# Attention matmuls in 64-row halves of the TensorE array, with ScalarE and VectorE in program order

## The chip, the cores and the metric

One core of one Trainium2 chip runs the whole program. The metric is device time in microseconds (us), lower is better: the median of three runs of the kernel before is 1672.16 us (1672.11 to 1676.5).

## The reference

Eight sequences of 2496 tokens go through an attention without softmax, then all 19968 tokens through a soft mixture of experts. Everything is float32.

```python
scores = (1.0 / S) * np.matmul(z, z.transpose(0, 2, 1))   # z: 8 x 2496 x 64
attn = np.maximum(scores, 0.0) ** 2
x = u * np.matmul(attn, v)                                # u, v: 8 x 2496 x 256
...
logits = x.reshape(N, D) @ phi                            # phi: 256 x 32 (8 experts, 4 slots each)
d = exp(logits - logits.max(0)); d /= d.sum(0) + 1e-9     # over the tokens
slot_out[e] = np.maximum((d.T @ x)[e] @ w1[e], 0) @ w2[e]
c = exp(logits - logits.max(1)); c /= c.sum(1) + 1e-9     # over the slots
out = c @ slot_out
```

## The kernel before, in words

**Split numbers.** Float32 products are made from the fast type fp32r: a value is split in a high part (a copy cast to fp32r) and a low part (the value less the high one), and a product is the sum of high x high, high x low and low x high. A tile of z holds both parts in both halves of its 128 rows: slot 0 has the high part in rows 0 to 63 and the low part in rows 64 to 127, slot 1 the other way round (`load_z`, L55 to L63). A tile of v holds high and low side by side (`load_v`, L65 to L71; its low part is made on GpSimd for 35 of the 80 tiles, L70).

**Attention.** A step is one tile of 128 keys (`kt`, 20 of them) for one chunk of up to 512 queries (`ch`; five per sequence, four of 512 and one of 448 columns, and in the last sequence six, the last two of 256). `scores` (L134) makes a 128 x 512 tile of scores with two matmuls over all 128 rows (L141, L142: they give all four products, low x low too), ScalarE takes relu (L144) and square (L145), VectorE casts the high part `ph` (L147) and subtracts the low part `pl` (L150). `attend` (L156) then adds six matmuls over all 128 rows (keys) to the accumulator `acc`, two column halves c of v by three products (L163 four, L169 two). `scores` runs three steps ahead of `attend` (LOOKAHEAD). The last key tile has 64 real keys; its high and low parts share one tile, so it needs four matmuls in `attend`.

**Small steps.** A finished chunk is multiplied by u, split in `xh` and `xl` (`finish_chunk`, L178), and for each group of 512 tokens g a list `work` gets four `group_tile` calls (L201: transposition of 128 tokens and their logits in one matmul by `rmat`, `tr`, L209, then copies) and four stages of `group_soft` (L224: the running maximum over tokens by two transpositions, `cmT` L238 and `mbT` L250, exponentials L254, L271, L281, and the sums over the slots `sl`, eight matmuls L263 and L264). One entry of `work` is taken at each of eight places of a chunk (POPS).

**Order.** The Tile scheduler sets the order on each engine by priority; nothing is pinned but one pair (`issue_after`). PSUM: `acc` has two buffers of two banks, `sc` two of one bank, `ms` (the small steps) two of one bank.

**End.** The turning of the weights c (`turn`, L287), the expert layers (L405, L427) and the output (`tokens`, L473). The last are matmuls over 32 rows each, four of them in four different row strips of the array (L481), with their own weights, 512 columns wide, type fp32r.

Of the kernel before, what the change touches and what calls it, by code (L numbers as in the profile page):

```python
# [15 lines left out]
P = 128  # L16
# [11 lines left out]
LOOKAHEAD = 3  # L28
# [3 lines left out]
STAGES = 4  # L32
POPS = (3, 5, 7, 9, 11, 13, 16, 18)
# [5 lines left out]

@with_exitstack  # L40
def attn_soft_moe_kernel(ctx, tc, uT, v, zz, phi, ww, outT):
    nc = tc.nc

# [4 lines left out]
    ms_ps = mid_ps.enter_context(tc.tile_pool(name="ms_ps", bufs=2, space=PSUM))  # L48
# [3 lines left out]
    xpool = moe.enter_context(tc.tile_pool(name="xpool", bufs=1))  # L52


    def load_z(b, j):  # L55
        raw = raws.tile([P, 512], F32, tag="raw", name=f"zr_{b}_{j}")
        nc.sync.dma_start(raw, zz[b, :, j * 512 : (j + 1) * 512])
        t = blk.tile([P, 2, 512], F32R, tag="blk", name=f"z_{b}_{j}")
        for h in (1, 0):
            rows = slice(h * 64, (h + 1) * 64)  # L60
            (nc.vector.tensor_copy if h and b + j == 0 else nc.scalar.copy)(t[rows, h], raw[rows])
            nc.vector.tensor_sub(t[rows, 1 - h], raw[rows], f32(t[rows, h]))  # L62
        return t  # L63

    def load_v(b, i):  # L65
        raw = raws.tile([P, 2, D], F32, tag="raw", name=f"vr_{b}_{i}")
        nc.sync.dma_start(raw, v[b, :, 2 * i : 2 * i + 2, :])
        t = blk.tile([P, 2, 2, D], F32R, tag="blk", name=f"v_{b}_{i}")
        nc.scalar.copy(t[:, :, 0], raw)  # L69
        (nc.gpsimd if b and i > 4 else nc.vector).tensor_sub(t[:, :, 1], raw, f32(t[:, :, 0]))  # L70
        return t  # L71

    zt, vt_ = {(0, 0): load_z(0, 0)}, {}


    ident = cpool.tile([P, P], F32, name="ident")
    make_identity(nc, ident)


    esel = cpool.tile([2 * NS, E_, NS], F32, name="esel")  # L80
    rsel = cpool.tile([P, 2, 4, NS], F32, name="rsel")
    nc.gpsimd.memset(esel, 0.0)
    nc.gpsimd.memset(rsel, 0.0)
    for h in range(2):
        rows = slice(h * NS, (h + 1) * NS)
        nc.gpsimd.tensor_copy(
            esel[rows, :, 0:SE], ident[rows, rows].rearrange("k (e s) -> k e s", s=SE)
        )
        for r in range(4):
            nc.gpsimd.tensor_copy(  # L90
                rsel[:, h, r, 16 * h : 16 * h + 16].rearrange("k (j s) -> k j s", s=SE),
                ident.rearrange("k (j q) -> k j q", q=NS)[:, :, 0:SE],
            )
    phi_sb = xpool.tile([P, 2, NS], F32, name="phi_sb")
    nc.sync.dma_start(phi_sb, phi.rearrange("(c p) s -> p c s", p=P))
    rmat = xpool.tile([P, 2, 256], F32R, name="rmat")
    nc.vector.memset(f32(rmat), 0.0)
    for c in range(2):
        nc.vector.tensor_copy(rmat[:, c, 0:P], ident)
        nc.vector.tensor_copy(rmat[:, c, P : P + NS], phi_sb[:, c])  # L100
        nc.vector.tensor_sub(
            rmat[:, c, P + NS : P + 2 * NS], phi_sb[:, c], f32(rmat[:, c, P : P + NS])
        )


    NXT = 6
    xth = [xpool.tile([P, 258], F32R, name=f"xth{i}") for i in range(NXT)]
    xtl = [xpool.tile([P, 256], F32R, name=f"xtl{i}") for i in range(NXT)]
    for t in xth:
        nc.vector.memset(f32(t[:, 256:258]), 1.0)  # L110
    slot_acc = [cpool.tile([2 * NS, 258], F32, name=f"slot_acc{i}") for i in range(2)]
    runmax = [cpool.tile([2 * NS, 1], F32, name=f"runmax{i}") for i in range(2)]
    cw = cpool.tile([P, NG, P], F32, name="cw")
# [19 lines left out]

    pend = {}  # L134

    def scores(b, ch, kt):
        j, o, n, t0 = ch
        zk, zq = zt[b, kt // 4], zt[b, j]
        ps = sc_ps.tile([P, QC], F32, tag="sc", name=f"sc_{t0}_{kt}")
        lhs = zk[:, 0, (kt % 4) * P : (kt % 4 + 1) * P]  # L140
        nc.tensor.matmul(ps[:, :n], lhs, zq[:, 0, o : o + n], start=True, stop=False)  # L141
        nc.tensor.matmul(ps[:, :n], lhs, zq[:, 1, o : o + n], start=False, stop=True)  # L142
        r = wa.tile([P, QC], F32, tag="r", name=f"r_{t0}_{kt}", bufs=4)
        nc.scalar.activation(r[:, :n], ps[:, :n], AF.Relu, scale=1.0 / S)  # L144
        nc.scalar.activation(r[:, :n], r[:, :n], AF.Square)  # L145
        hi = wa.tile([P, QC], F32R, tag="ph", name=f"ph_{t0}_{kt}", bufs=5)
        nc.vector.tensor_copy(hi[:, :n], r[:, :n])  # L147
        if kt < KT - 1:
            lo = wa.tile([P, QC], F32R, tag="pl", name=f"pl_{t0}_{kt}", bufs=5)
            nc.vector.tensor_sub(lo[:, :n], r[:, :n], f32(hi[:, :n]))  # L150
        else:
            lo = None
            nc.vector.tensor_sub(hi[64:128, :n], r[64:128, :n], f32(hi[64:128, :n]))  # L153
        pend[t0, kt] = hi, lo

    def attend(b, ch, kt, acc):  # L156
        j, o, n, t0 = ch
        hi, lo = pend.pop((t0, kt))
        vt = vt_[b, kt // 2][:, kt % 2]
        last = kt == KT - 1  # L160
        for c in range(2):
            for h in range(2):
# [392 lines left out]
```

## Time and profile before

| what | value |
|---|---|
| profiled execution, its own time | 1676.33 us |
| its span, first to last instruction | 1674.6 us |
| runs | 1676.5, 1672.11, 1672.16 us |
| granted TensorE clock, mean | 0.986 |
| busy: PE, VectorE (DVE), ScalarE (ACT), GpSimd (POOL) | 1632.9, 1296.0, 1154.1, 58.4 us |
| matmuls, other instructions of note | 8155 matmuls, each with a weight load (PEld); 216 DMAs |
| HBM | 53 GB/s over the span |

How to read the profile's rows. A group row names line, engine, operation, output<-inputs, shape, xcount, then busy us, mean ns of one, and the idle time ahead of it with what ended it. A timeline row has the start in us from the span's start, the length, and xcount instructions merged. Matmuls are pipelined: a 512-column matmul is shown with about 390 ns, but the next one starts some 230 ns after it, so distances between starts are what counts. A row of windows has the length of a stretch and the busy time (and count) of each engine in it.

### The profile page before, as it was taken

What the parts mean: (1) busy time and instruction counts of PE and PEld (TensorE: products, weight loads), DVE (VectorE), ACT (ScalarE), POOL (GpSimd) and SP (SyncE); (2) the same over time, 40 slices, a digit from 0 to 9 for tenths busy, and PEclk for the clock granted to TensorE, in tenths of its full rate; (3) what the DMA queues carried; (4) which work ended last, traced back from release to release, by engine and by line L of the source; (5) the groups of instructions that cost most, each with busy time, mean ns of one, the idle gap of its engine ahead of it and who ended that gap; (6) DMA issues with size and microseconds to landing.
All of it is one profiled execution on the core that took longest, in us unless ns stands there. A gap on an engine that the chain in (4) does not pass through costs nothing.

```text
span 1674.6 us, 22717 instructions
## 1 busy us (share of the span) xinstructions
PE 1632.9 (98%) x8155; PEld 1347.3 (80%) x8155; DVE 1296.0 (77%) x2904; ACT 1154.1 (69%) x2191; POOL 58.4 (3%) x53
## 2 busy tenths in 40 slices
PE   8999999999999999999999999999999999999985
PEld 6788888888888888888888888888888889888953
DVE  8877977779777887779877797778977787777853
ACT  8766866678666776668666686667866676666743
POOL 0000100000000100001000010001000020000000
PEclk9999999999999999999999999999999999999985
DMA  5100310013000120002100030001200021000559
GB/s 158 51 14 12 89 44 14 11 32 89 13 14 12 57 63 14 13 12 77 44 13 14 18 100 27 14 12 45 76 13 14 12 81 63 13 15 12 182 222 389
DMA packets 36594, 90.63 MB, mean 54 GB/s; under 512 B 3713, under 2 KB 6273, under 8 KB 34433
## 3 DMA queue, kind: packets, MB, share of 16 engines
q1 hardware_dynamic: 36480, 89.18, 16.4%
q8 instruction: 64, 1.05, 0.3%
q14 instruction: 50, 0.40, 0.1%
HBM read 68.71 MB, written 20.45 MB: 53 GB/s over the span
## 4 chain that ended last, share of the span: by engine, by line
PE 88%; DVE 6%; ACT 2%; DMA 2%; issue 1%; SPq 0%; DVEq 0%; ACTq 0%
PE acc L163 40%; PE acc L169 19%; PE sc L141 10%; PE sc L142 10%; PE tr L209 4%; DVE pl L150 2%; DMA outT<-ot 2%; DVE ph L147 2%; PE sl L263 1%; PE sl L264 1%; DVE z L62 1%; ACT r L145 1%; ACT r L144 1%; PE h L405 1%; DVE ot L487 1%
## 5 line engine op out<-in xcount | busy, mean ns | idle before, releaser
L163 PE MATMUL acc<-ph,v 128*128 128x512 f32 (+2 forms) x3280 | 862.5, 385 | 0.3 <-DVE ph L153 0.3
L144 ACT ACTIVATE r<-sc 128x512 f32<-128x512 f32 (+2 forms) x820 | 471.5, 575 | 407.5 <-PE sc L142 402.9
L163 PEld LDWEIGHTS acc<-ph,v 128*128 128x128 f32 x3280 | 608.7, 188 | 123.3 <-DVE ph L153 0.7
L150 DVE TENSOR_TENSOR pl<-r,ph 128x512 fp32r<-128x512 f32 (+2 forms) x779 | 528.3, 679 | 23.8
L147 DVE CAST ph<-r 128x512 fp32r<-128x512 f32 (+2 forms) x820 | 345.8, 423 | 221.0 <-ACT r L145 210.4
L145 ACT ACTIVATE r<-r 128x512 f32<-128x512 f32 (+2 forms) x820 | 502.1, 612 | 16.8
L169 PE MATMUL acc<-pl,v 128*128 128x512 f32 (+2 forms) x1558 | 472.0, 384 | 0.0
L169 PEld LDWEIGHTS acc<-pl,v 128*128 128x128 f32 x1558 | 290.3, 188 | 57.8
L141 PE MATMUL sc<-z,z 128*128 128x512 f32 (+2 forms) x656 | 258.2, 394 | 0.0
L142 PE MATMUL sc<-z,z 128*128 128x512 f32 (+2 forms) x656 | 251.4, 383 | 0.0
L141 PEld LDWEIGHTS sc<-z,z 128*128 128x128 f32 x656 | 123.5, 188 | 21.8
L142 PEld LDWEIGHTS sc<-z,z 128*128 128x128 f32 x656 | 123.7, 189 | 17.2
L221 DVE TENSOR_TENSOR xtl<-tr,xth 128x256 fp32r<-128x256 f32 x156 | 65.5, 420 | 51.4 <-ACT xth L220 51.3
L70 POOL TENSOR_TENSOR v<-vr,v 128x512 fp32r<-128x512 f32 x35 | 55.7, 1605 | 1314.4 <-ACT v L69 942.3
L209 PE MATMUL tr<-rmat,xl 128*128 128x256 f32 x312 | 80.5, 281 | 0.0
L209 PE MATMUL tr<-rmat,xh 128*128 128x256 f32 x312 | 80.3, 280 | 0.0
L220 ACT CAST xth<-tr 128x256 fp32r<-128x256 f32 x156 | 57.4, 369 | 20.9 <-DVE lt L215 20.6
L141 PE MATMUL sc<-z 128*128 128x512 f32 (+2 forms) x164 | 65.9, 402 | 5.9 <-DVE z L62 4.7
L142 PE MATMUL sc<-z 128*128 128x512 f32 (+2 forms) x164 | 63.9, 390 | 0.3 <-DVE z L62 0.3
L209 PEld LDWEIGHTS tr<-rmat,xh 128*128 128x128 f32 x312 | 58.6, 188 | 5.8
L209 PEld LDWEIGHTS tr<-rmat,xl 128*128 128x128 f32 x312 | 58.5, 188 | 5.6 <-DVE xl L193 0.2
L191 DVE TENSOR_TENSOR x<-acc,ut 128x256 f32<-128x256 f32 (+7 forms) x72 | 52.3, 727 | 5.7 <-PE acc L163 5.7
(88 smaller groups left out, 954.3 us busy)
## 6 DMA issues: line engine op xcount, KB each, us to landing
vr<-in_v SPq DMA_DIRECT2D x80, 256.0 KB, 2.7
w<-in_w SPq DMA_DIRECT2D x32, 512.0 KB, 6.0
outT<-ot SPq DMA_DIRECT2D x16, 1024.0 KB, 8.4
ut<-in_uT SPq DMA_DIRECT2D x31, 512.0 KB, 3.7
zr<-in_zz SPq DMA_DIRECT2D x40, 256.0 KB, 2.6
ut<-in_uT SPq DMA_DIRECT2D x8, 448.0 KB, 3.4
outT<-ot SPq DMA_DIRECT2D x4, 512.0 KB, 5.1
outT<-ot SPq DMA_DIRECT2D x2, 768.0 KB, 6.0
```

What stands on the lines that cost most here:

```text
L70: (nc.gpsimd if b and i > 4 else nc.vector).tensor_sub(t[:, :, 1], raw, f32(t[:, :, 0]))
L141: nc.tensor.matmul(ps[:, :n], lhs, zq[:, 0, o : o + n], start=True, stop=False)
L142: nc.tensor.matmul(ps[:, :n], lhs, zq[:, 1, o : o + n], start=False, stop=True)
L144: nc.scalar.activation(r[:, :n], ps[:, :n], AF.Relu, scale=1.0 / S)
L145: nc.scalar.activation(r[:, :n], r[:, :n], AF.Square)
L147: nc.vector.tensor_copy(hi[:, :n], r[:, :n])
L150: nc.vector.tensor_sub(lo[:, :n], r[:, :n], f32(hi[:, :n]))
L163: nc.tensor.matmul(acc[:, c, :n], vt[:, h, c * P : (c + 1) * P], hi[:, :n], start=(kt == 0 and h == 0), stop=(last and h == 1),)
L169: nc.tensor.matmul(acc[:, c, :n], vt[:, 0, c * P : (c + 1) * P], lo[:, :n], start=False, stop=False,)
L209: nc.tensor.matmul(ps[:, c], xp[:, c, t * P : (t + 1) * P], rmat[:, c], start=(k == 0), stop=(k == 1))
L220: nc.scalar.copy(xth[i][:, 0:D].rearrange("p (c q) -> p c q", c=2), ps[:, :, 0:P])
L221: nc.vector.tensor_sub(xtl[i].rearrange("p (c q) -> p c q", c=2), ps[:, :, 0:P], f32(xth[i][:, 0:D]).rearrange("p (c q) -> p c q", c=2),)
```

## The change

Line numbers of the changed kernel are of no use below, since all its operations are recorded through one helper (L46), so tile names are used: `sc` scores, `ph`/`pl` high and low part of the squared scores, `acc` the accumulator, `tr`, `cmT`, `mbT`, `sl` the small steps.

1. **Scores.** Two key tiles at a time: tile h (0 or 1) uses rows 64h to 64h+63 of z only, with three matmuls over 64 rows (high x high, high x low, low x high; low x low is dropped). The two halves alternate, each into its own bank.
2. **Attend.** Four key tiles (p) at a time, in two passes s. Each matmul over 128 keys becomes two over 64 keys. In pass s the half h writes column half c = h XOR s, so that the two halves are always in different banks. Between the passes a GpSimd no-op waits for the last matmul of a pass, and the first matmul of the next pass waits for that no-op (`turns`, `await_`).
3. **Order.** Everything recorded through `pe`, `act`, `dve` keeps the order of the code. Ahead of each pass s stand one entry of `work` and the scores of the pair after (`pair(i + 1, s)`); three lists (`begin`, `middle`, `behind`) put each small ScalarE or VectorE step half a step after its input.
4. **Small steps.** `tr`, `cmT`, `mbT` in 64-row halves; `sl` in plain float32 as eight matmuls of 64 rows by 32 columns (four token tiles by two halves) instead of eight fp32r matmuls over 128 rows; `ms` has one buffer of two banks; logits and `xt` are copied by ScalarE; the low part of x for `sl` and its copies go away; the low part of v is made on VectorE always.
5. **Loads.** The DMAs stay on SP's queue in much the same places; the split of a loaded tile is put one load later (`landing`); at the start the constants come after the first scores.
6. The very last block of attention is done over 128 rows (`attend_whole`). The expert layers and the output are unchanged.

```diff
-    def scores(b, ch, kt):
+    def scores(b, ch, p, w):
...
-        nc.tensor.matmul(ps[:, :n], lhs, zq[:, 0, o : o + n], start=True, stop=False)
-        nc.tensor.matmul(ps[:, :n], lhs, zq[:, 1, o : o + n], start=False, stop=True)
+        for m, (kl, ql) in enumerate(((0, 0), (0, 1), (1, 0))):
+            for h, rows in enumerate(HALF):
+                c = 2 * w + h
+                pe.matmul(
+                    ps[h][:, :n], zk[rows, h ^ kl, c * P : (c + 1) * P],
+                    zq[rows, h ^ ql, o : o + n], start=(m == 0), stop=(m == 2),
+                )
+        rs = []
+        for h in range(2):
+            r = wa.tile([P, QC], F32, tag="r", name=f"r_{t0}_{k0 + h}", bufs=5)
+            act.activation(r[:, :n], ps[h][:, :n], AF.Relu, scale=1.0 / S)
+            rs.append(r)
+        run(middle)
+        for kt, r in enumerate(rs, k0):
+            act.activation(r[:, :n], r[:, :n], AF.Square)
+            hi = wa.tile([P, QC], F32R, tag="ph", name=f"ph_{t0}_{kt}", bufs=7)
+            dve.tensor_copy(hi[:, :n], r[:, :n])
...
+        run(behind)
+
+    def attend(b, ch, p, acc, between):
...
+        for s in range(2):
+            between(s)
+            before = turns[-1:]
+            for i in range(len(todo[0])):
+                for h, rows in enumerate(HALF):
...
+                    vp, pp = todo[h][i]
+                    c = h ^ s
+                    x = pe.matmul(
+                        acc[:, c, :n], vp[rows, c * P : (c + 1) * P], pp[rows, :n],
+                        start=(p == 0 and s == 0 and i == 0),
+                        stop=(p == NP - 1 and s == 1 and i == len(todo[h]) - 1),
+                    )
+                    while before:
+                        await_(x, before.pop())
+            turns.append(nc.gpsimd.nop())
+            await_(turns[-1], x)
...
         for t in range(4):
-            i = (g * 4 + t) % NXT
-            dt = dd[:, t].rearrange("p h s -> p (h s)")
-            nc.tensor.matmul(psl[0 : 2 * NS, 0:258], dt, xth[i], start=(t == 0), stop=False)
-            nc.tensor.matmul(psl[0 : 2 * NS, 0:256], dt, xtl[i], start=False, stop=(t == 3))
+            for h, rows in enumerate(HALF):
+                pe.matmul(
+                    psl[t * NS : (t + 1) * NS, h, 0:258], ex[rows, t],
+                    xt[(g * 4 + t) % NXT][rows], start=True, stop=True,
+                )
...
+        def between(s):
+            run(begin)
+            if work and 2 * p + s > 1:
+                work.pop(0)()
+            pair(i + 1, s)
```

TensorE before, in the middle of a chunk of the fifth sequence, one step: two matmuls of scores three steps ahead, then six into `acc`. A wait behind a row is for an engine's semaphore.

```order
L141 MATMUL sc_10_9010<-z_1_7246,z_2_7333 128x512 [waits Activation_49]
L142 MATMUL sc_10_9010<-z_1_7246,z_2_7333 128x512
L163 MATMUL acc_8889<-ph_6_8936,v_3_7845 128x512 [waits DVE_49]
L163 MATMUL acc_8889<-ph_6_8936,v_3_7845 128x512 x3
L169 MATMUL acc_8889<-pl_6_8938,v_3_7845 128x512 [waits DVE_49]
L169 MATMUL acc_8889<-pl_6_8938,v_3_7845 128x512
```

TensorE of the change at a like place, one pass s = 1 of four key tiles: the scores of the pair ahead (three half matmuls for each of two key tiles, taking turns), then 24 half matmuls into `acc`, all with inputs that the pass s = 0 has used before.

```order
L46 MATMUL sc_6_7711<-z_3_4649,z_1_4394 128x512
L46 MATMUL sc_7_7712<-z_3_4649,z_1_4394 128x512
L46 MATMUL acc_7649<-ph_0_7550,v_0_4882 128x512 [waits Pool_sequencer_49]
L46 MATMUL acc_7649<-ph_0_7550,v_0_4882 128x512 x3
L46 MATMUL acc_7649<-pl_0_7552,v_0_4882 128x512 x2
L46 MATMUL acc_7649<-ph_1_7555,v_0_4882 128x512 x4
L46 MATMUL acc_7649<-pl_1_7557,v_0_4882 128x512 x2
L46 MATMUL acc_7649<-ph_2_7614,v_1_4992 128x512 x4
L46 MATMUL acc_7649<-pl_2_7616,v_1_4992 128x512 x2
```

Per four key tiles there are now 12 half matmuls of scores and 48 into `acc`, where there were 8 and 24 whole ones; new is the wait for GpSimd's sequencer (the no-op) at the head of each pass, with only the scores of a pair, and at some passes an entry of `work`, between it and the matmul that the no-op waits for.

TensorE before, at the end of a group: `mbT` (32 rows) and, four steps later, the eight matmuls of `sl`.

```order
L169 MATMUL acc_8060<-pl_11_8223,v_5_6000 128x448 x2
L250 MATMUL mbT_8291<-ident,mb_8252 128x32
L141 MATMUL sc_15_8299<-z_4_5428,z_3_5327 128x448
...
L169 MATMUL acc_8060<-pl_13_8262,v_6_6061 128x448 x2
L263 MATMUL sl_8331<-xth_114,dd_8296 64x258
L264 MATMUL sl_8331<-xtl_120,dd_8296 64x256
```

TensorE of the change there: `sl` with outputs of 32 rows, two half matmuls per token tile, directly ahead of the scores.

```order
L46 MATMUL acc_8832<-pl_11_9016,v_5_8434 128x512 x2
L46 MATMUL sl_9157<-xt_85,ex_9100 32x258 x2
L46 MATMUL sl_9157<-xt_86,ex_9100 32x258 x2
L46 MATMUL sl_9157<-xt_81,ex_9100 32x258 x2
L46 MATMUL sl_9157<-xt_82,ex_9100 32x258 x2
L46 MATMUL sc_16_9172<-z_0_7192,z_4_7677 128x512
```

ScalarE before, around a group's exponentials (`al`, `ex`, `cw`): they stand between the relu and the square of single tiles, where the scheduler found room.

```order
L271 ACTIVATE al_8747<-al_8747 64x1 [waits DVE_49]
L144 ACTIVATE r_14_8685<-sc_14_8682 128x512 [waits PE_49]
L145 ACTIVATE r_14_8685<-r_14_8685 128x512 [waits Activation_49]
L144 ACTIVATE r_15_8709<-sc_15_8706 128x512 [waits PE_49]
L254 ACTIVATE ex_8700<-ex_8700 128x128 [waits DVE_49]
L145 ACTIVATE r_15_8709<-r_15_8709 128x512 [waits Activation_49]
```

ScalarE of the change there: two relus, the three exponentials, two squares, and the cast of a loaded tile of v last.

```order
L46 ACTIVATE r_16_10906<-sc_16_10898 128x512 [waits DVE_49,PE_49]
L46 ACTIVATE r_17_10908<-sc_17_10899 128x512 [waits DVE_49,PE_49]
L46 ACTIVATE ex_10891<-ex_10891 128x128 [waits DVE_49]
L46 ACTIVATE al_10892<-al_10892 128x1 [waits DVE_49]
L46 ACTIVATE cw<-cw 128x128 [waits DVE_49]
L46 ACTIVATE r_16_10906<-r_16_10906 128x512 [waits Activation_49]
L46 ACTIVATE r_17_10908<-r_17_10908 128x512 [waits Activation_49]
L46 CAST v_2_10923<-vr_2_10730 128x2x256 [waits DMAHW7_49]
```

The relus, on which the next scores wait for their bank, stand ahead of everything else of a pass; a step that is late now holds all that follows on its engine.

More of the change, by code (lines that the diff above doesn't have):

```diff
@@ L27 @@
 ROT = S - QC * (NQ - 1)
-LOOKAHEAD = 3
+NP = KT // 4
 NBLK = 23
@@ L106, in attn_soft_moe_kernel @@
[L106 to L113, printed above, removed]
+                esel[rows, :, 0:SE], ident[rows, rows].rearrange("k (e s) -> k e s", s=SE)
+            )
@@ L361, in attn_soft_moe_kernel @@
+        if p == NP - 1:
+            finish_chunk(b, ch, acc)
+    for todo in (middle, behind, begin):
+        run(todo)
+    while work:
+        work.pop(0)()
+        for todo in (middle, behind, begin):
+            run(todo)
     att.close()
+    att_ps.close()
+    ms_ps = mid_ps.enter_context(tc.tile_pool(name="end_ps", bufs=2, space=PSUM))
     exx = ExitStack()
```

374 lines of the change are left out of this document (215 added, 159 removed).

## The prediction

> **What bounds the kernel.** The page's first parts say where to look.
>
> ```profile
> span 1674.6 us, 22717 instructions
> PE 1632.9 (98%) x8155; PEld 1347.3 (80%) x8155; DVE 1296.0 (77%) x2904; ACT 1154.1 (69%) x2191; POOL 58.4 (3%) x53
> PE 88%; DVE 6%; ACT 2%; DMA 2%; issue 1%; SPq 0%; DVEq 0%; ACTq 0%
> ```
>
> TensorE is busy 98% of the span and holds 88% of the chain that ended last. A share is an average, so the stages come next (windows: length, busy time and count by engine, granted clock, DMA).
>
> ```profile
> 16.06:1584.66 1568.60, 1559.38 (x7453) 1300.62 (x7452) 1242.31 (x2804) 1109.57 (x2120) 55.73 (x35) 1.00 0.13 38
> 1584.66:1595.44 10.78, 8.09 (x58) 6.05 (x56) 8.48 (x26) 4.82 (x12) 0.00 (x0) 1.00 1.01 387
> 1595.44:1674.60 79.16, 55.56 (x625) 34.06 (x625) 34.73 (x46) 29.39 (x42) 0.00 (x0) 0.69 0.73 299
> ```
>
> Attention with its small steps takes 1568.6 us, TensorE busy 99% of it at clock 1.00; the last group's tail is 10.8 us; the experts and the output, 79.2 us, are not changed. How fast does TensorE go? The timeline of one step:
>
> ```profile
> 799.81 0.39 PE L141 MATMUL sc<-z,z 128*128 128x512 f32 x1
> 800.04 0.40 PE L142 MATMUL sc<-z,z 128*128 128x512 f32 x1
> 800.28 1.09 PE L163 MATMUL acc<-ph,v 128*128 128x512 f32 x4
> 801.20 0.63 PE L169 MATMUL acc<-pl,v 128*128 128x512 f32 x2
> 801.67 0.40 PE L141 MATMUL sc<-z,z 128*128 128x512 f32 x1
> ```
>
> From one score matmul to the next are 1.86 us for eight matmuls: **0.2325 us a pass** of 512 columns, without a gap. So attention costs its number of passes, and only the waits below come on top.
>
> ```profile
> ACT r L144 <- PE sc L142: 402.9, 564, 1.7
> PE mbT L250 <- DVE al L270: 6.6, 5, 1.4
> PE sl L263 <- DVE dd L257: 3.4, 6, 1.2
> ```
>
> ScalarE waits 403 us for scores, TensorE only 10 us for the small steps.
>
> **The change, part by part.** Count first. One relu is one score tile; their forms give the widths (ScalarE and VectorE rows are used again below).
>
> ```profile
> L144 ACT ACTIVATE r<-sc 128x512 f32<-128x512 f32 x620 | 370.1, 597 | 364.0 <-PE sc L142 361.4 <-DVE ph L147 1.1
> L144 ACT ACTIVATE r<-sc 128x448 f32<-128x448 f32 x160 | 86.2, 539 | 35.1 <-PE sc L142 34.3 <-DVE pl L150 0.3
> L144 ACT ACTIVATE r<-sc 128x256 f32<-128x256 f32 x40 | 15.2, 381 | 8.4 <-PE sc L142 7.2
> L147 DVE CAST ph<-r 128x512 fp32r<-128x512 f32 x620 | 261.9, 423 | 202.0 <-ACT r L145 194.1
> L150 DVE TENSOR_TENSOR pl<-r,ph 128x512 fp32r<-128x512 f32 x589 | 405.2, 688 | 19.1
> ```
>
> That is 620 + 160 x 0.875 + 40 x 0.5 = 780 tiles of 512 columns.
>
> *Scores.* Two whole matmuls become three half ones. If two halves run side by side, a tile costs 1.5 passes, not 2: 780 x 0.5 x 0.2325 = **90.7 us less**. *Attend* splits each matmul in two halves: no pass is saved or added. In all 780 x 1.5 + 4602 = 5772 passes are left (4602 of attend: 5.9 a tile, six but four for every twentieth), if halves do pair. No half of 64 rows is in the trace; the nearest is the output stage, four matmuls of 32 rows in four strips, each with its own weights, 512 columns, the same type:
>
> ```profile
> 1634.88 0.30 PEld L481 LDWEIGHTS pf<-cp,soh 32*128 32x128 f32 x6 [0.91 <-DVE ot L487]
> 1634.89 0.74 PE L481 MATMUL pf<-cp,soh 32*128 32x512 f32 x6 [0.59 <-DVE ot L487]
> 1635.00 0.41 PEld L481 LDWEIGHTS pf<-cp,sol 32*128 32x128 f32 x4
> 1635.23 0.63 PE L481 MATMUL pf<-cp,sol 32*128 32x512 f32 x4
> ```
>
> These ten matmuls (a few records are missing; three groups of four) end at 1635.86, 0.97 us after the first began. Less the 0.39 us of one matmul and about 0.11 us for the first, open weight load (0.74 - 0.63) are 0.47 us for the two later groups: 0.235 us a group of four. Four strips go abreast at the pace of one, weights hidden, so I take two abreast at 0.2325 us. Bounds: nothing lost; or, if each pair showed its load as the first group does (1634.89 to 1635.23), 0.34 us.
>
> The Trainium skill gives a lower yield (TensorE: Matmul & The Clock Gate, Measured speedup vs the span model): four row tiles of K=32 at N=512 ran 3.07 times as fast, not four times. By that a pass would cost 0.2325 x 4 / 3.07 = 0.303 us, an estimate, and the kernel some 400 us more than my sum. The trace disagrees, with 0.235 us for a group of four.
>
> *Small steps.* `mbT` is now a matmul of 32 rows amid matmuls of 128:
>
> ```profile
> 1018.80 0.63 PE L169 MATMUL acc<-pl,v 128*128 128x512 f32 x2
> 1019.36 0.24 PE L250 MATMUL mbT<-ident,mb 32*128 32x32 f32 x1
> 1019.53 0.51 PE L141 MATMUL sc<-z,z 128*128 128x512 f32 x1
> 1019.87 0.40 PE L142 MATMUL sc<-z,z 128*128 128x512 f32 x1
> ```
>
> Without it L142 would start three passes after 1018.80, at 1019.50; it starts at 1019.87. So `mbT` costs 0.37 us, nearly all of it for going to another tiling and back. In 64 rows it keeps the tiling of its neighbours, about 0.06 us: 39 x 0.31 = 12 us less (0 to 14). `sl` is the reverse: eight matmuls of 258 columns, 8 x 0.117 = 0.94 us, become eight float32 ones in tiles of 64 x 32, with the two changes of tiling, 0.31 us. Their own time is bounded by the expert layer:
>
> ```profile
> 1604.52 1.92 PE L405 MATMUL h<-w,sT 128*32 128x512 f32 x16
> ```
>
> Eight float32 matmuls (two records each), four abreast, in 1.92 us; half the columns make 0.97 us. Eight abreast would make 0.48, one after another 3.9. Rows and columns are each seen side by side, so I take 0.6: 0.6 + 0.31 - 0.94, no change (-6 us at 0.48, +13 at 0.97, the far end +127). `tr` keeps its passes. The 10 us of waits fell mostly at batch edges, where GpSimd made parts of v; I count 6 of them gone (0 to 10).
>
> *Waits added.* At each of some 408 passes the first `acc` matmul waits for the no-op, and 23 half matmuls and the next scores queue behind it; ScalarE waits for those. Hops in the trace:
>
> ```profile
> 18.15 0.40 PE L142 MATMUL sc<-z,z 128*128 128x512 f32 x1
> 18.58 0.60 ACT L144 ACTIVATE r<-sc 128x512 f32<-128x512 f32 x1 [0.15 <-PE sc L142]
> 181.09 0.60 ACT L69 CAST v<-vr 128x512 fp32r<-128x512 f32 x1
> 181.77 1.66 POOL L70 TENSOR_TENSOR v<-vr,v 128x512 fp32r<-128x512 f32 x1 [1.56 <-ACT v L69]
> 1633.61 1.22 DVE L487 COPY ot<-pf 128x1024 f32<-128x1024 f32 x1
> ```
>
> A consumer starts 0.43 us after a matmul's start (18.15 to 18.58); GpSimd 0.08 us after what it waited for (181.69 to 181.77); TensorE's load 0.05 us after VectorE's end (1634.83 to 1634.88, above). The round takes 0.43 + 0.08 + 0.05 = 0.56 us, with no row for the no-op itself. Meanwhile three passes of scores run: the load is due 3 x 0.2325 = 0.70 us after the last matmul's start at 512 columns, 0.61 at 448, 0.35 at 256. Hidden at the first two, 0.2 us late in the last sequence's 20 narrow passes: 4 us. Bounds: 0, and 50 us if the no-op adds 0.2 us (0.06 to 0.15 us late at 408 places).
>
> *Program order.* A pass is 12 + 3 half pairs, 15 x 0.2325 = 3.49 us. ScalarE's part by two rows:
>
> ```profile
> 9.19 1.06 ACT L144 ACTIVATE r<-sc 128x512 f32<-128x512 f32 x2
> 10.14 1.15 ACT L145 ACTIVATE r<-r 128x512 f32<-128x512 f32 x2
> 6.50 1.26 ACT L61 CAST z<-zr 64x512 fp32r<-64x512 f32 x2
> 4.74 0.76 PE L141 MATMUL sc<-z 128*128 128x512 f32 x1 [4.74 <-DVE z L62]
> ```
>
> Two relus and two squares are 2.21 us; with a tile of z, 3.47; with the two copies after `tr` (under 0.74), 4.2 us, while such a pass has `tr`'s 0.47 us more on TensorE, 3.96. The next scores need only the relus, done 0.2 + 1.06 us after the last ones, and are due 12 passes, 2.79 us, later: 1.5 us in hand, which an overrun of 0.25 us doesn't spend. VectorE has 2 x (0.423 + 0.688) = 2.22 us a pass, plus 1.4 for z; `ph` and `pl` of a pair are read from 12 + 3 + 6 passes (4.9 us) after its scores, and ready after 0.2 + 1.06 + 1.15 + 1.1 = 3.5. So both are hidden; if that cover went, each lost 0.1 us a pass would be 41 us. I put 5 us for chunk and batch edges (0 to 25). SP's DMAs keep their order; a raw tile's split comes one load later, with four raw buffers. The low part of v, 35 x 0.68 = 24 us more on VectorE, fits its idle time.
>
> *Start and tail.* The first score matmul began at 4.74 and the stream ran evenly from 16.06 (windows above). Now the first `acc` matmul needs four score tiles, two of v and the next z, in order: +3 us (0 to 5). The last group's steps run one after another with one `ms` buffer: +2 us (0 to 5).
>
> Sum: -90.7 + 0 - 12 - 6 + 4 + 5 + 3 + 2 = **-94.7 us**. The profiled execution took 1676.33 us, so 1581.6; it stands 4.2 us above the median of the runs, hence 1577.5, say **1578 us**.
>
> **Rivals.**
> - *The handshake shows.* For: GpSimd's own step has no row, and the cover is 0.14 us at 512 columns, 0.05 at 448. Against: passes with `work` have up to 0.47 us more. At 0.12 us a pass, 408 x 0.12 = 49: 1627 us.
> - *ScalarE or VectorE falls behind.* For: in order, one late step holds all; passes with z and `tr` exceed their time. Against: the 1.5 us in hand. At 0.1 us a pass, 41 us: 1619 us.
> - *Pairs don't close up (slower).* Place: every pair in attention. If the second half's load or start isn't hidden, a pass grows; from 94.7 / 5772 = 0.016 us more, 0.249 us, the change loses. At 0.34 us, 1578 + 5772 x 0.11 = 2213 us. For: no 64-row half in the trace, and loads double. Against: four abreast at 0.235.
> - That the halves might not be built: the order rows show them.
>
> **How the numbers follow.** Forecast 0.66 (1562 to 1595, its terms' small bounds), handshake 0.13, falling behind 0.10, pairs 0.08, about no change 0.03. A measurement here tells some 0.3% from none. Faster 0.89, within 0.03, slower 0.08. The range runs to 1636: it holds the forecast and most of the first two rivals, and leaves out the slower one.
>
> **What the changed profile would show.** Right: pairs of half matmuls starting within 0.02 us, 0.23 us from pair to pair; `acc` groups with no idle time put down to POOL; ScalarE still waiting for scores. Handshake: idle ahead of the first `acc` matmul of a pass. Behind: `sc` waiting for ACT. Wrong altogether: pairs 0.25 us apart or more. `sl` above 1.3 us would make its term wrong.

## The result: 5% faster, and where the profile after shows it

| | before | changed |
|---|---|---|
| median of four runs each | 1674.32 us (1672.11 to 1676.5) | 1590.95 us (1588.58 to 1592.8) |
| ratio, 95% interval | | 0.9501 [0.9477, 0.9525] |
| profiled execution, its own time | 1676.33 us | 1589.23 us, 87.1 less |
| mean granted TensorE clock | 0.986 | 0.984 |

The changed kernel is faster. The prediction, 1578 us with a range of 1562 to 1636, was right in direction, in its mechanism and in its range; between the two profiled executions it had 94.7 us, and 87.1 came. First the page of the changed kernel: its span, the busy times, and the shares of the chain that ended last.

```profile
span 1587.4 us, 37236 instructions
PE 1534.9 (97%) x14686; PEld 1300.1 (82%) x14686; DVE 1258.0 (79%) x2714; ACT 1103.6 (70%) x2346; POOL 3.3 (0%) x20
PE 86%; DVE 7%; DMA 2%; ACT 2%; issue 2%; DVEq 0%; SPq 0%; ACTq 0%
```

TensorE is still the bound. It has nearly twice the matmuls and is busy 98 us less: that is what two half matmuls side by side look like. GpSimd's 35 parts of v are gone, and its no-ops leave no rows.

To see where the time went, both executions are cut at the same places of the program: where VectorE begins the product of a finished chunk with u (`x<-acc,ut`), for the first chunk, for the last one ahead of the two narrow ones, and for the last of all. Windows of the kernel before (length, busy time and count of PE, PEld, DVE, ACT, POOL, then granted clock, DMA share, GB/s):

```profile
0.00:52.01 52.01, 45.52 (x175) 35.05 (x176) 45.07 (x92) 44.98 (x81) 2.68 (x18) 1.00 0.52 152
52.01:1543.90 1491.89, 1482.98 (x6960) 1231.66 (x6959) 1172.96 (x2636) 1043.26 (x1971) 55.73 (x35) 1.00 0.11 33
1543.90:1584.87 40.97, 40.97 (x345) 40.64 (x344) 34.77 (x108) 31.65 (x85) 0.00 (x0) 1.00 0.42 138
1584.87:1674.60 89.73, 63.44 (x681) 39.90 (x679) 43.21 (x71) 34.20 (x54) 0.00 (x0) 0.73 0.76 310
```

The same four stretches of the changed kernel:

```profile
0.00:61.73 61.73, 44.09 (x321) 32.07 (x323) 40.97 (x85) 37.80 (x70) 3.34 (x20) 1.00 0.32 99
61.73:1456.69 1394.96, 1387.56 (x13057) 1190.90 (x13055) 1141.70 (x2469) 1003.53 (x2135) 0.00 (x0) 1.00 0.13 37
1456.69:1498.35 41.66, 39.70 (x619) 37.62 (x618) 32.62 (x99) 27.63 (x89) 0.00 (x0) 1.00 0.40 135
1498.35:1587.40 89.05, 63.59 (x698) 39.51 (x696) 42.72 (x66) 34.67 (x55) 0.00 (x0) 0.72 0.77 313
```

So the first chunk takes **9.7 us more**, the 38 chunks after it **96.9 us less**, the two narrow ones 0.7 more, the rest 0.7 less: together 87.2 us, the difference of the spans. The start is where the prediction lost its accuracy.

In the long stretch TensorE runs as forecast. Timeline of one pass:

```profile
701.49 0.64 PE L46 MATMUL acc<-ph,v 64*128 64x512 f32 x4
701.96 0.40 PE L46 MATMUL acc<-pl,v 64*128 64x512 f32 x2
702.19 0.86 PE L46 MATMUL sc<-z 64*128 64x512 f32 x6
702.88 0.63 PE L46 MATMUL acc<-ph,v 64*128 64x512 f32 x4
```

Six half matmuls go from 701.49 to 702.19 and six from there to 702.88, 0.70 and 0.69 us: three turns of 0.233 us for three pairs. A pair costs what one whole matmul cost.

### The profile page after: what moved, and what is told of

Its sections match the earlier page's. It is cut to its first block, busy times and chain, and to the rows that moved or that the text cites. A ratio compares the mean times of both kernels' runs of the same rounds, so it can differ in the third digit from the quotient of the medians.

```text
span 1587.4 us, 37236 instructions
## 1 busy us (share of the span) xinstructions
PE 1534.9 (97%) x14686; PEld 1300.1 (82%) x14686; DVE 1258.0 (79%) x2714; ACT 1103.6 (70%) x2346; POOL 3.3 (0%) x20
## 4 chain that ended last, share of the span: by engine, by line
PE 86%; DVE 7%; DMA 2%; ACT 2%; issue 2%; DVEq 0%; SPq 0%; ACTq 0%
PE acc L46 62%; PE sc L46 16%; PE tr L46 5%; DMA outT<-ot 2%; DVE z L46 2%; DVE ph L46 1%; PE sl L46 1%; ACT r L46 1%; DVE pl L46 1%; PE h L542 1%; DVE x L46 0%; PE po L564 0%; DVE slot_acc L46 0%; DVE ot L624 0%; DVE v L46 0%
## 5 line engine op out<-in xcount | busy, mean ns | idle before, releaser
L46 PE MATMUL acc<-ph,v 64*128 64x512 f32 (+2 forms) x6464 | 1094.8, 382 | 0.7 <-DVE ph L46 0.7
L46 PEld LDWEIGHTS acc<-ph,v 64*128 64x128 f32 x6464 | 782.1, 184 | 90.3 <-DVE ph L46 1.8
L46 PE MATMUL acc<-pl,v 64*128 64x512 f32 (+2 forms) x3110 | 789.6, 381 | 0.0
L46 ACT ACTIVATE r<-sc 128x512 f32<-128x512 f32 (+2 forms) x820 | 428.4, 575 | 264.2 <-PE sc L46 253.1
L46 DVE TENSOR_TENSOR pl<-r,ph 128x512 fp32r<-128x512 f32 (+2 forms) x779 | 519.0, 666 | 51.8 <-PE acc L46 0.5
L46 DVE CAST ph<-r 128x512 fp32r<-128x512 f32 (+2 forms) x820 | 334.9, 408 | 205.4 <-ACT r L46 202.2
L46 PEld LDWEIGHTS acc<-pl,v 64*128 64x128 f32 x3110 | 448.0, 184 | 46.6 <-DVE pl L46 2.0
L46 ACT ACTIVATE r<-r 128x512 f32<-128x512 f32 (+2 forms) x820 | 455.2, 611 | 0.0
L46 PE MATMUL sc<-z,z 64*128 64x512 f32 (+2 forms) x1968 | 325.3, 389 | 12.4 <-ACT z L46 7.3
L46 PEld LDWEIGHTS sc<-z,z 64*128 64x128 f32 x1968 | 213.4, 185 | 44.8 <-issue 12.9
L46 ACT COPY lg<-tr 128x128 f32<-128x128 f32 x156 | 41.2, 264 | 124.6 <-PE tr L46 124.2
L46 PE MATMUL tr<-rmat,xl 64*128 64x256 f32 x624 | 100.0, 281 | 5.5 <-DVE xl L46 5.4
L46 PE MATMUL tr<-rmat,xh 64*128 64x256 f32 x624 | 101.6, 280 | 1.3 <-DVE slot_acc L46 1.3
L46 PEld LDWEIGHTS tr<-rmat,xh 64*128 64x128 f32 x624 | 84.9, 184 | 9.9 <-PE acc L46 3.3
L46 PE MATMUL sc<-z 64*128 64x512 f32 (+2 forms) x492 | 82.8, 395 | 5.3 <-ACT z L46 4.1
L46 PEld LDWEIGHTS tr<-rmat,xl 64*128 64x128 f32 x624 | 74.5, 184 | 10.8 <-DVE xl L46 8.5
L46 PEld LDWEIGHTS sc<-z 64*128 64x128 f32 x492 | 53.9, 188 | 13.6 <-ACT z L46 4.1
L46 DVE TENSOR_REDUCE lt<-lg 128x32 f32<-128x128 f32 x156 | 59.7, 383 | 0.8 <-ACT lg L46 0.5
L46 ACT COPY xt<-tr 128x256 f32<-128x256 f32 x156 | 59.0, 378 | 0.0
L46 DVE TENSOR_TENSOR v<-vr,v 128x512 fp32r<-128x512 f32 x80 | 54.8, 686 | 4.1 <-ACT v L46 3.8
L46 ACT CAST v<-vr 128x512 fp32r<-128x512 f32 x80 | 49.4, 617 | 12.0 <-PE sc L46 12.0
L46 DVE TENSOR_TENSOR z<-zr,z 64x512 fp32r<-64x512 f32 x80 | 55.0, 687 | 2.5
```

What stands on the lines that cost most here:

```text
L46: return lambda *a, **k: self.tc.keep_in_program_order(f(*a, **k))
```

## The experiments

Theory: the gain is the scores' half passes, plus small steps that stay in the tiling of their neighbours; the no-op and program order cost nothing in the steady part; the start pays for program order. Rivals: the no-op's round shows; program order costs time everywhere; the gain hangs on other things (GpSimd's parts of v, the order in which halves take turns).

### Scores over all 128 rows again

```diff
-        for m, (kl, ql) in enumerate(((0, 0), (0, 1), (1, 0))):
-            for h, rows in enumerate(HALF):
-                c = 2 * w + h
+        for h in range(2):
+            c = 2 * w + h
+            for m in range(2):
                 pe.matmul(
-                    ps[h][:, :n], zk[rows, h ^ kl, c * P : (c + 1) * P],
-                    zq[rows, h ^ ql, o : o + n], start=(m == 0), stop=(m == 2),
+                    ps[h][:, :n], zk[:, 0, c * P : (c + 1) * P], zq[:, m, o : o + n],
+                    start=(m == 0), stop=(m == 1),
                 )
```

> The changed kernel with the scores of before: two matmuls over all 128 rows for a key tile, everything else in halves. Theory: 0.5 passes more for each of 780 tiles, 90.7 us, and a way to another tiling and back in each of 407 passes; the small transpose that is one (the run before: 0.28 us less its own 0.02 to 0.06, so 0.22 to 0.31) gives 90 to 126 us. Together 1591 + 181 to 217 = 1772 to 1808 us, slower than the kernel before (1673). Rival, going between 64 and 128 rows is free since the number of columns is the same: 1591 + 91 = 1682 us, about the kernel before.

Measured (two runs): 1806.25 us, ratio 1.079 [1.0763, 1.0818]; 215 us more than the changed kernel. The timeline at the change from 64 rows to 128 and back:

```profile
900.70 0.28 PE L46 MATMUL tr<-rmat,xl 64*128 64x256 f32 x2
900.91 1.20 PE L46 MATMUL sc<-z,z 128*128 128x512 f32 x4
902.03 0.73 PE L46 MATMUL acc<-ph,v 64*128 64x512 f32 x4
902.60 0.40 PE L46 MATMUL acc<-pl,v 64*128 64x512 f32 x2
```

The scores would be due 0.117 us after the last `tr`, at 900.82, and start at 900.91; `acc` would be due four turns later, at 901.84, and starts at 902.03; its first four halves take 0.57 us where 0.47 is usual. Of the 215 us, 90.7 are the passes; the other 125 us over 407 passes are 0.31 us for each way to the other tiling and back. The theory's upper end is met, and the rival, a free change of tiling, falls. It also says why all attention work had to change at once: scores in 128 rows amid halves are slower than the kernel before.

### `mbT` with 32 rows again

```diff
-        pe.transpose(pb[:, 0, 0:64], mb, ident[0:64, 0:64])
+        pe.transpose(pb[:, 0, 0:32], mb[0:32], ident[0:32, 0:32])
```

> The changed kernel, but mbT is one transpose of 32 rows again, as in the kernel before, amid matmuls of 64 rows. Theory: going to another tiling and back costs 0.31 us at each of 39 places, so 12 us more, 1603 us, and the phases with mbT take 0.3 us more in the trace. Rival, a 32-row matmul amid 64-row halves costs nothing beyond its own 0.06 us (only the way from 128 rows is dear): 1591 us.

Measured: 1598.87 us, ratio 0.9559 [0.9545, 0.9574]; by the medians 7.9 us more. The place in the changed kernel, then in this one:

```profile
709.05 0.40 PE L46 MATMUL acc<-pl,v 64*128 64x512 f32 x2
709.29 0.21 PE L46 MATMUL mbT<-ident,mb 64*128 64x64 f32 x1
709.29 0.96 PE L46 MATMUL sc<-z,z 64*128 64x512 f32 x6
```

```profile
716.26 0.40 PE L46 MATMUL acc<-pl,v 64*128 64x512 f32 x2
716.59 0.24 PE L46 MATMUL mbT<-ident,mb 32*128 32x32 f32 x1
716.77 0.96 PE L46 MATMUL sc<-z,z 64*128 64x512 f32 x6
```

The scores are due 0.23 us after the last pair's start. In the changed kernel they come then, `mbT` in the shadow of one half; here they come 0.28 us late. 39 x 0.28 would be 11 us; the run shows 7.9, and from the end of the first chunk to the start of the last product this trace needs 1442.4 us against 1436.6, 5.8 more. So it is shown that a 32-row transposition amid halves costs 6 to 8 us. The forecast's 12 us were read from the kernel before, where it stands amid whole matmuls; that size this run does not measure.

### The handshake made longer

```diff
-            turns.append(nc.gpsimd.nop())
+            turns.append(nc.gpsimd.memset(flag, 0.0))
```

In a second run three memsets stand there: the first waits for the last matmul of the pass, and the next pass waits for the third.

> The changed kernel, but GpSimd's no-op between two passes is a memset of one element, which leaves a row in the trace. Theory: the no-op's round (about 0.56 us by the rows of before) is over before the weight load that waits for it is due (0.70 us after the last matmul's start at 512 columns, 0.61 at 448, 0.35 at 256). A memset may take up to the 0.19 us of GpSimd's 128x16 copy; the round is then at most 0.75 us, late by 0.05 us at some 308 passes of 512 columns, 0.14 at 79 of 448, 0.40 at 20 of 256: 0 to 34 us more than the changed kernel's 1591 us, 1591 to 1625. Rival, the no-op's round is already late: every tenth of a microsecond shows at all 408 passes, 1591 + 408 x 0.19 = 1668 us at 0.19, and the rows of the loads in the changed kernel must then show a gap ahead of the first acc matmul of a pass.

> The same with three memsets one after the other, the third awaited. Theory: at 0.19 us each the round is 1.13 us, late by 0.43 us at 308 passes, 0.52 at 79, 0.78 at 20: 189 us more, 1780 us; at 0.1 us each the round is 0.86, late by 0.16, 0.25 and 0.51 us: 79 us more, 1670 us. The slope from one to three memsets at 512 columns is then the whole of two memsets, and what is missing from one to none is the cover. Rival, the wait is not on TensorE's path at all (another wait always ends later): no change at one and at three.

Measured: one memset 1594.53 us, ratio 0.9531 [0.9516, 0.9546], not told apart from the changed kernel by the intervals; three 1631.06 us, ratio 0.975 [0.9736, 0.9765], 40 us more. What the weight loads of `acc` waited for, with one memset and with three (us in total, times, longest):

```profile
PEld acc L46 <- POOL flag L247: 11.6, 49, 0.3
```

```profile
PEld acc L46 <- POOL flag L248: 85.1, 208, 0.6
```

In the changed kernel's waits no load of `acc` waits for GpSimd. Its no-op has no row, but the page of the profile has only 0.7 us of idle time ahead of the 6464 matmuls of `acc` with `ph`, and that for VectorE:

```profile
L46 PE MATMUL acc<-ph,v 64*128 64x512 f32 (+2 forms) x6464 | 1094.8, 382 | 0.7 <-DVE ph L46 0.7
```

So the no-op is covered, with about one memset (a mean of 183 ns) to spare; the wait is real, since at three memsets it costs 0.1 us a pass. Some 200 of the 407 passes show no wait even then. "The handshake shows" falls. The run with one memset came out near the low end of what was expected, the one with three below it: half of the single memsets take only 88 ns, and the cover is larger than the 0.14 us that I had worked out.

### Free order on ScalarE and VectorE

```diff
-    pe, act, dve = (InOrder(tc, x) for x in (nc.tensor, nc.scalar, nc.vector))
+    pe, act, dve = InOrder(tc, nc.tensor), nc.scalar, nc.vector
```

> The changed kernel without program order on ScalarE and VectorE (TensorE keeps it): the scheduler places their instructions. Theory: in the steady part both engines have time in hand, so nothing changes there; it gains only at the start, where program order puts the next z behind v: between 0 and 8 us less, 1583 to 1591 us. Rival, program order is what keeps relus and parts in time: small steps and splits placed ahead of them make the scores or acc wait, 0.1 us a pass is 41 us, 1632 us.

Measured: 1620.29 us, ratio 0.9679 [0.9657, 0.9702], 29 us **more**. My theory falls here, and the rival is right in kind. The timeline at a change of sequence shows how:

```profile
380.39 3.83 ACT L78 CAST z<-zr 64x512 fp32r<-64x512 f32 x6
...
382.58 2.83 DVE L79 TENSOR_TENSOR z<-zr,z 64x512 fp32r<-64x512 f32 x4
...
384.13 0.96 ACT L201 ACTIVATE r<-sc 128x448 f32<-128x448 f32 x2
...
386.45 0.41 DVE L395 TENSOR_TENSOR slot_acc<-slot_acc,sl 128x258 f32<-128x258 f32 x1
...
387.00 0.39 PE L46 MATMUL tr<-rmat,xh 64*128 64x256 f32 x2 [3.65 <-DVE slot_acc L395]
```

The scheduler puts six casts for three tiles of z in a row on ScalarE, 3.83 us, the relus behind them. VectorE's subtractions for these tiles stand ahead of its last step on `sl` (`slot_acc`), `tr` needs the bank of `sl`, and TensorE stands for 3.65 us. From the first chunk's product to the last TensorE's own waits add up to 28.0 us, against 9.3 in the changed kernel. The waits are not all: at six of the seven changes of sequence the granted clock then falls to about half, for 3.4 us at five of them and 6.8 at one, 24 us in all. One of them (windows; granted clock in the third column from the right):

```profile
388.24:391.66 3.42, 3.42 (x22) 3.42 (x20) 2.60 (x6) 3.31 (x8) 0.00 (x0) 0.51 0.12 44
```

At half the clock that is some 12 us of work more, an estimate. With TensorE's order fixed, a burst of splits on another engine has nothing that evens it out; written order spreads it, one tile a pass. So program order on ScalarE and VectorE is worth 29 us here, about two thirds of it waits and one third the clock. I had it as a cost of 5.

### Before, with all low parts of v on VectorE

```diff
-        (nc.gpsimd if b and i > 4 else nc.vector).tensor_sub(t[:, :, 1], raw, f32(t[:, :, 0]))
+        nc.vector.tensor_sub(t[:, :, 1], raw, f32(t[:, :, 0]))
```

> The kernel before with all low parts of v on VectorE, none on GpSimd, as the change has it. Theory: the waits of mbT and sl at batch edges, 10 us in the trace of before, came of GpSimd's part beside VectorE's work; 6 of them go (0 to 10): 1673 - 6 = 1667 us. Rival, VectorE's 35 x 0.68 = 24 us more in these chunks make the waits longer: 1673 us or more.

Measured: 1664.87 us beside 1672.80 for the kernel before, ratio 0.9946 [0.993, 0.9963]. The theory holds, with 7.9 us instead of 6. The wait of `mbT`, 6.6 us before, is no longer listed, and that of `sl`, 3.4 before, is down to this:

```profile
PE sl L263 <- DVE dd L257: 1.3, 2, 1.0
```

So some 8 us of the change's gain have nothing to do with halves.

### The start: z split ahead of v

What TensorE waited for in the changed kernel (us in total, times, longest):

```profile
PE sc L46 <- ACT z L46: 11.4, 5, 4.1
...
PE sc L46 <- DVE z L46: 5.5, 5, 1.4
PE tr L46 <- DVE xl L46: 5.4, 6, 1.7
```

All five of each of the first two lie in the first chunk, the first of them at the very first scores. One of its steps in the timeline:

```profile
22.98 0.62 ACT L46 CAST v<-vr 128x512 fp32r<-128x512 f32 x1
...
23.62 1.25 ACT L46 CAST z<-zr 64x512 fp32r<-64x512 f32 x2
...
24.93 0.73 PE L46 MATMUL sc<-z,z 64*128 64x512 f32 x4 [1.20 <-ACT z L46]
...
25.52 1.40 DVE L46 TENSOR_TENSOR z<-zr,z 64x512 fp32r<-64x512 f32 x2
...
26.98 0.50 PE L46 MATMUL sc<-z,z 64*128 64x512 f32 x2 [1.32 <-DVE z L46]
```

The scores of a pair need the z that is split last, behind the pair's relus and squares and behind v. TensorE waits 1.20 us for its high parts, then 1.32 for the low ones. Two orders of the splits were tried, the second on top of the first:

```diff
-        opening += [(load_v, 2 * p), (load_v, 2 * p + 1)] + [(load_z, p + 1)] * (p + 1 < NP)
+        opening += [(load_z, p + 1)] * (p + 1 < NP) + [(load_v, 2 * p), (load_v, 2 * p + 1)]
```

> The changed kernel, but in the first chunk the split of the next z comes ahead of the two tiles of v, not behind them. The first chunk of the changed kernel ends (its product with u starts) at 61.73 us, in the kernel before at 52.01, though it has 2.3 us less of scores. Theory: 9 to 10 of these 12 us are the scores' waits for the z that is split last, 1.2 us for ScalarE's half and 1.3 us for VectorE's, at each of four key steps, because program order puts v, the relus and the squares ahead of it. With z first the first chunk ends 6 to 10 us earlier, and so does the kernel: 1581 to 1585 us. Rival, ScalarE's and VectorE's sum of work bounds the first chunk: the order makes no difference, 1591 us, and the waits move to the acc matmuls, for v.

```diff
-        if i < NP:
+        if i < NP and (opening or opened):
             next_split()
-            if w and opened:
+            if not w and opened:
                 next_split()
```

> As the run with z first, but in the first chunk the next z and one tile of v are split behind the first pair of a step, the second v behind the second pair. With z first, TensorE still waited 0.9 to 1.3 us a step for the low part of v (VectorE), at three steps. Theory: these three waits go, 3 us less than with z first, 1580 us; more isn't to be had there, since ScalarE's and VectorE's work of such a step is 7.0 and 7.2 us against TensorE's 6.98. Rival, ScalarE's first half of a step (two relus, two squares, z and v, 4.1 us against TensorE's 3.49) then delays the scores as much: 1583 us.

Measured: z first 1583.09 us, ratio 0.9465 [0.9449, 0.9481], the first chunk's product at 55.5 us; z and one v 1580.44 us, ratio 0.9444 [0.9428, 0.946], its product at 51.86:

```profile
51.86 1.22 DVE L46 TENSOR_TENSOR x<-acc,ut 128x1024 f32<-128x1024 f32 x1
```

Both theories are met. 9.9 us of the first chunk, against 61.73, came of the places of the splits in the written order: 6.2 of the z's, 3.7 of one v's. The medians fell by 10.5 us.

### z's low parts behind xl

```diff
-                dve.tensor_sub(t[rows, 1 - h], raw[rows], f32(t[rows, h]))
+                if b == 0:
+                    dve.tensor_sub(t[rows, 1 - h], raw[rows], f32(t[rows, h]))
+                else:
+                    begin.append(lambda rows=rows, h=h: dve.tensor_sub(t[rows, 1 - h], raw[rows], f32(t[rows, h])))
```

> The run before this one (z and one v behind the first pair), and in all later sequences the low parts of z go behind xl on VectorE, not ahead of it. In the changed kernel's trace tr waits for xl 11 times (8.5 us of weight loads, 5.4 of matmuls), where a z was split just ahead of it. Theory: these waits go, 5 to 8 us less: 1573 to 1577 us. Rival, something else is late in these passes (ScalarE's copies for xh, one z tile of 1.26 us behind them): no more than 2 us less.

Measured: 1576.45 us, ratio 0.9420 [0.9406, 0.9434]; 4 us less than the run above, a little less than expected. TensorE's own wait for xl went from 5.4 us to:

```profile
PE tr L46 <- DVE xl L46: 1.5, 4, 0.6
```

This version beats both kernels: 14.5 us less than the changed one, 5.8% less than the one before.

### The order in which halves take turns

```diff
-        for m, (kl, ql) in enumerate(((0, 0), (0, 1), (1, 0))):
-            for h, rows in enumerate(HALF):
+        for h, rows in enumerate(HALF):
+            for m, (kl, ql) in enumerate(((0, 0), (0, 1), (1, 0))):
```

> The changed kernel, the same matmuls, but the three score matmuls of the lower half first, then the three of the upper half. Theory: TensorE starts matmuls in program order, and a half goes beside another only if its neighbour in that order is in the other half. The three of the lower half then take three turns, the first of the upper half goes beside the third, its third beside the first of acc; every pass is one turn of 0.2325 us longer: 407 passes, 398 of full width, 93 us, 1684 us. Rival, the two halves have queues of their own and the order between them doesn't matter: 1591 us.

Measured (two runs): 1594.65 us, ratio 0.9526 [0.9504, 0.9548]. My theory falls. From the first chunk's product to the last this trace needs 1436.7 us (66.83 to 1503.49), the changed kernel 1436.6. A timeline there:

```profile
707.41 0.86 PE L46 MATMUL sc<-z 64*128 64x512 f32 x6
708.10 0.64 PE L46 MATMUL acc<-ph,v 64*128 64x512 f32 x4
```

Six matmuls, written three and three, take 0.69 us: three turns. The first of the upper half, fourth in program order, starts with the first of the lower. How far does that reach? The same for the 12 `acc` matmuls of a half, and then in groups of four:

```diff
-            for i in range(len(todo[0])):
-                for h, rows in enumerate(HALF):
-                    if i >= len(todo[h]):
-                        continue
+            for h, rows in enumerate(HALF):
+                for i in range(len(todo[h])):
```

```diff
-            for i in range(len(todo[0])):
-                for h, rows in enumerate(HALF):
-                    if i >= len(todo[h]):
-                        continue
+            for h, i in [(h, i) for g in (0, 4, 8) for h in (0, 1) for i in range(g, min(g + 4, len(todo[h])))]:
+                for rows in HALF[h : h + 1]:
```

> The changed kernel with the 12 acc matmuls of the lower half of a pass first, then the 12 of the upper half. The run with three scores of one half ahead of three of the other fell on the side of the rival: 1594.65 us, no turn lost. The question is now how far one half can run ahead of the other in the queue. Theory: only a few, about the three or four seen there: of 12 turns alone 8 to 9 are lost at the start of a pass, and as many at its end are shared with what follows only as far as that reach: 8 to 12 turns of 0.2325 us at 398 passes, 740 to 1110 us more, 2330 to 2700 us. Rival, a half has a long queue of its own: 1591 to 1600 us.

> The changed kernel with the acc matmuls of a pass in groups of four of one half: four lower, four upper, four lower and so on. With twelve of one half ahead of the other, the first of the upper half started together with the eighth of the lower: four were still waiting behind that one. Theory: a matmul may start ahead of program order past up to four waiting ones of the other half; in fours only three stand in between, so nothing is lost: 1591 to 1600 us. Rival, the reach differs from place to place or each change of half costs a turn: three to five turns of 0.2325 us in each of 398 passes, 280 to 460 us more, 1870 us or more.

Measured: in twelves (one run) 2186.99 us, 596 more than the changed kernel; in fours (two runs) 1593.99 us, ratio 0.9515 [0.9476, 0.9553], 3 us more, which the intervals don't tell apart. In the run with twelves, TensorE's matmuls of `acc` in two stretches of one pass (length, busy time and count, clock, DMA):

```profile
903.87:905.50 1.63, 1.62 (x7) 1.00 0.07 15
905.50:906.43 0.93, 0.93 (x9) 1.00 0.00 0
```

This pass holds the last key tile, so the lower half has eleven matmuls and the upper ten. The lower goes alone for seven turns, 1.63 us. The first of the upper half starts with its eighth, at 905.51, when three of the lower are still to come behind that one; from there they go two by two, eight matmuls in 0.93 us (the count of nine holds one that began before). In passes with twelve the starts show eight turns alone, and again three still to come. So the expectation of the run in fours counted one too many: the reach is three waiting matmuls, not four, and in fours just three stand in between. A few matmuls it is, as expected; the loss was 6.4 turns a pass (596 / 398 / 0.2325), less than the 8 to 12 that I gave, because at its end the upper half's last matmuls go beside the next scores.

## Why the prediction came out as it did

| term | predicted, us | measured, us, and from what |
|---|---|---|
| scores | -90.7 | -90.7 fits: a pair takes 0.233 us, and 215 us come back with whole scores |
| `sl` | 0 | -6, by the rows below |
| `mbT` | -12 | -6 to -8, by the run with 32 rows; with `sl` about -15, by the two traces below |
| waits | -6 | -8, by the kernel before with v on VectorE |
| handshake | +4 | no wait for it; the narrow chunks lost 3.0 (2.3 less of scores, yet 0.7 longer), 1.9 of it waits for VectorE |
| program order, edges | +5 | +9 to +12, what is left of the long stretch |
| start | +3 | +12.0 (9.7 longer, with 2.3 less of scores) |
| tail | +2 | -0.7 |

*What bounds the kernel; scores; attend.* Right. In the 38 chunks from 61.73 to 1456.69 the scores save 780 - 20 - 20 = 740 tile widths x 0.5 x 0.2325 = 86.0 us. With 6 for `sl`, 6 for `mbT` and 8 for the waits that is 106; 96.9 were measured, so some 9 us were lost at edges (12, if `mbT` and `sl` saved 15). TensorE's own waits in this stretch add up to 7.4 us, all for VectorE: `tr` for `xl` 4.8, `cmT` for `cm` 1.3, `tr` for `slot_acc` 1.3. The run with z's low parts behind xl got 4 back.

*`sl`.* The rows in the changed kernel:

```profile
712.56 0.49 PE L46 MATMUL acc<-pl,v 64*128 64x512 f32 x2
712.98 0.67 PE L46 MATMUL sl<-xt,ex 64*32 64x258 f32 x16
713.57 0.96 PE L46 MATMUL sc<-z,z 64*128 64x512 f32 x6
```

The scores were due at 712.79 and start at 713.57: 0.78 us, where 0.6 + 0.31 = 0.91 was forecast and 0.94 was spent before. 39 x 0.16 = 6 us less. `mbT` and `sl` can also be read together: from the last `acc` ahead of `mbT` to the first behind `sl`, nineteen passes apart in both kernels, are 5.73 us before and 5.32 changed (medians of 29 places with 512 columns). That is 0.41 us a place, some 15 us in all.

*Handshake.* The 4 us forecast for the narrow passes did not come as a wait. TensorE's own waits in these chunks are for VectorE's `ph` (0.7 us), `cm` (0.6) and `xl` (0.6); in the run with one memset, which has a row, no load of these chunks waits for it. What made the other 1.1 us is open.

*Start.* **This is the step that failed**, though the forecast as a whole came true: "Now the first `acc` matmul needs four score tiles, two of v and the next z, in order: +3 us (0 to 5)." I costed one wait at the beginning. But that z is a new one at each of the first chunk's steps, and program order puts it last each time: 1.2 + 1.3 us at three more places, after a first one that was longer. From one such wait to the next are 10.05 us (24.93 to 34.98) instead of two passes of 3.49, so 3.1 us are lost three times, 9.2 of the 12.0. The 1.5 us in hand that I worked out for the relus were no cover for it, since in this chunk ScalarE has a z and two v more to do in each step. The written order (the list `opening`, in the diff above) has the z's place; I didn't lay a step of the first chunk against its durations as I did a steady one. The two runs with another order of the splits show the cause: 9.9 us of the chunk.

*Rivals.* Pairs close up (0.233 us). The handshake is covered. "ScalarE or VectorE falls behind" happened, in the first chunk and, much smaller, at the places where TensorE waits for `xl`, `cm` and `slot_acc` (7.4 us). The lower yield that the Trainium skill gives (TensorE: Matmul & The Clock Gate, Measured speedup vs the span model) for four tiles of 32 rows did not occur with two halves: a turn of the two takes 0.233 us, the time of one whole matmul.

## What to carry to other kernels

A matmul that uses half the rows is worth splitting off only if its neighbours are in halves too: here each change of tiling and back cost 0.31 us, more than the 0.23 us that the scores of two key tiles save. When an order is written out, lay its first round against the durations as well as a steady one, since its loads and splits come together there; one split moved ahead gave 8 us. And a wait's cover is measured well by making the wait longer step by step: one memset showed little, three showed 40 us.

## What the runs showed of the hardware

**Half matmuls may start ahead of program order.** Three or four of one half ahead of the other cost 3 to 4 us at most (1594.65 and 1593.99 us beside 1590.95); of twelve, the other half starts when three are still waiting (2186.99 us). The Trainium skill says otherwise (TensorE: Matmul & The Clock Gate, The mechanism): matmuls start and end strictly in program order. The rows of these runs disagree, for matmuls of different row halves.

**A memset of one element waits for VectorE's cast.** Rows of the run with one memset:

```profile
766.04 0.69 DVE L46 TENSOR_TENSOR pl<-r,ph 128x512 fp32r<-128x512 f32 x1
...
766.61 0.09 POOL L247 MEMSET flag<- 1x1 f32 x1 [3.40 <-PE acc L46]
```

```profile
770.45 0.42 DVE L46 CAST ph<-r 128x512 fp32r<-128x512 f32 x1
...
770.57 0.34 POOL L247 MEMSET flag<- 1x1 f32 x1 [3.87 <-PE acc L46]
```

Begun during a subtraction it takes 0.09 us; begun during a cast it ends 0.04 us after the cast, at 770.91. Of 213 memsets that begin when VectorE's latest instruction is a `ph` cast, still running, 178 take over 0.15 us; of 126 that begin so in a `pl` subtraction, none. The Trainium skill (SBUF — State Buffer, SBUF: two separate sides) states that VectorE and GpSimd share a port pair that one instruction holds to its end, and that a VectorE instruction with two inputs contends only with a GpSimd one that reads SBUF, which a memset does not; these rows agree.

**Waits of TensorE can halve its clock.** The run with free order showed it at changes of sequence; it happens at the start as well. In the run with `mbT` in 32 rows, from the wait at 37 us on (windows; granted clock in the third column from the right):

```profile
37.00:43.00 6.00, 5.66 (x26) 4.44 (x28) 3.04 (x6) 2.63 (x5) 0.00 (x0) 0.50 0.30 84
43.00:50.00 7.00, 4.58 (x36) 3.13 (x32) 4.01 (x7) 3.87 (x7) 0.00 (x0) 0.98 0.17 44
```

Its first chunk ended at 66.26 us instead of 61.73, and that of the run with uninterleaved scores at 66.83, with a clock of 0.53 from 28 to 34 us. The changed kernel's own profiled execution has 1.00 there. So in these executions the late z cost 4 to 5 us more than the waits themselves. The Trainium skill (TensorE: Matmul & The Clock Gate, What's actually happening) has the clock at half after an idle window of about 3.4 us, whose place in time is not tied to the kernel's start; the waits at the start are shorter, 2.6 us within 3.5, and halved it in some executions only.
